# A new order at three seams of an expert layer, and twelve products into a bank that nobody reads

## The chip, the cores and the metric

The kernel runs on one core of a Trainium2 chip. The metric is the device time of one execution in microseconds. Engines are named as in the profile: PE is TensorE, DVE is VectorE, ACT is ScalarE, POOL is GpSimd, SP issues most of the DMAs; ACT and POOL have queues of their own, and POOL's gathers and scatters go through queue q0, SP's transfers through q1.

## The reference, cut to what matters

Three layers follow each other. Attention gives 2304 rows of 512. A mixture of 8 experts then adds to a row, if its skip score is positive, the output of the one expert with the largest gate value:

```python
do_compute = x @ w_skip > 0
xc = x[do_compute]
logits = xc @ w_gate
e_idx = np.argmax(logits, axis=1)
gate_w = probs[np.arange(len(xc)), e_idx]          # probs: softmax of logits
for e in range(E):                                 # E = 8
    mask = e_idx == e
    h = np.maximum(xc[mask] @ w1[e], 0.0)          # 512 x 1024
    y[mask] = gate_w[mask, None] * (h @ w2[e])     # 1024 x 512
out[do_compute] = xc + y
```

A third layer applies `h = x @ w_in; g = h * sigmoid(1.702 h); g @ w_out` to all rows (512 to 2048 to 512).

## The kernel before, in words

All products are made in float16 from two parts: a matrix is scaled by a power of two, its high part is `wh`, the rest `wl`; a product is high by high, low by high and high by low, added up in float32. The same holds for the rows (`xh`, `xl`) and for the hidden values (`hh`, `hl`).

The work has three stages. The first, to about 161 us, is attention in 16 units with the routing behind it: it writes the rows to a table `xd` (L644), the gate values to the same table (L755), and counts for each token the slot in its expert's list (`slots`, L729 to 731; `sa`, L723). A planner (class `Plan`) sets the order of all engines there, SP's among them, from a table of durations and priorities; loads of expert weights are handed to it as `fill`, each with the transfers that it must follow. `in_order` writes the order down as dependencies.

The second stage, to about 335 us, is the experts. For each expert two gathers bring 128 and 64 rows of its list (`gather`, L1017; row numbers `idt` and `idu`, L766 to 769), TensorE transposes them (`xprep`, L1030 and L1033, into `px`), ACT and DVE make `xh` and `xl`, and four blocks each of `l1` (`ph`, L1063) and `l2a`, `l2b` (`py`, L1086, L1101) follow with `l1h`, `l1l` (`hh`, `hl`) between. Each expert's weights are four loads of 1 MB (`load`, L935, key: expert, layer, half). For each half ACT takes a sum of squares (`bound`, `jk`, L951), TensorE adds it over the partitions (`scale`, `psw`, L62), DVE makes the power of two (`scb`, `w_e` to `w_s`, L75 to 81) and then `hi` (`wh`, ACT L975 or DVE L977) and `lo` (`wl`, L983) follow. `ymx`, `yrow`, `yadd` and `scatter` finish the rows.

The order of the second stage on PE, ACT, DVE and POOL is that of one sorted list: each step of expert e stands at e plus a number from the table `STAGE_B`, with exceptions in `head`, `mine` and `tail`, and extra steps that are appended. SP's order comes from the scheduler. Lines on which the change acts:

```python
head = dict(hi00=-6.0, hi01=-5.99, lo00=-5.98)
sched.append((-1.0, -2, 0, lambda e: passes()))
for _, e, i, fn in sorted(sched, key=lambda z: z[:3]):
    fn(e)
```

`passes` counts how many further passes the lists need: a product over the counts (`pc`, L1147), four operations on DVE (`cnt`, `gt`, `sums`, `tot`, L1148 to 1156); `count` reads the result on the engines (L1160) for a branch behind the experts. `xb0` to `xb4` (L774 to 789) find the one scale of all rows (`sx`). `ex.first` keeps the first `lo` behind the row numbers. `win.load`, `win.high`, `win.join` and `win.square` prepare the third layer's first weights beside the experts (ACT `w`, L252; DVE `w`, L231 to 233; ACT `jw`, L256); `win.wh[0]` is ready since the first stage.

The third stage runs from about 338 us to the end.

## Time and profile before

| what | value |
|---|---|
| three runs | 725.91, 728.62, 729.83 us (median 728.62) |
| profiled execution | 728.87 us, its span 727.2 us |
| mean granted clock of TensorE | 0.960 |
| PE busy | 654.9 us (90%) |
| DVE busy | 494.4 us (68%) |
| ACT busy | 425.6 us (59%) |
| POOL busy | 221.5 us (30%) |
| DMA, mean over the span | 131 GB/s |

The span runs from the first to the last instruction of the profiled execution. The granted clock is a share of TensorE's full speed: 1.00 is 2.4 GHz and 0.50 is 1.2 GHz. The busy shares are means over three stages with different limits, so the stretches around the changed places are shown by themselves further down. A release in brackets ("[5.41 <-PE pc L1147]") is the idle time before an instruction and what ended it; "issue" is a wait that the profile does not explain.

### The profile page before, as it was taken

To read this page: it belongs to the slowest core of one execution; us is meant where nothing else is said; L and a number is where in the kernel's file an instruction comes from. 1 tells how busy PE (TensorE), PEld (TensorE's weight loads), DVE (VectorE), ACT (ScalarE), POOL (GpSimd) and SP (SyncE) were. 2 spreads that over 40 slices of the span, in tenths; PEclk is the share of its full clock that TensorE was granted. 3 is DMA by queue.
4 is the path that set the end of the run, shared out by engine and by line. 5 is a ranking of instruction groups with operands and counts; after the bars stand their busy time and mean duration, and the time that the engine had idled before them with its cause. 6 is when DMAs were issued, how large, how long until landed. Compare 5 with 4: busy or idle time off the path is not lost.

```text
span 727.2 us, 16364 instructions
## 1 busy us (share of the span) xinstructions
PE 654.9 (90%) x6639; PEld 460.9 (63%) x6639; DVE 494.4 (68%) x1027; ACT 425.6 (59%) x891; POOL 221.5 (30%) x216
## 2 busy tenths in 40 slices
PE   4788988773889999975999999999999999999997
PEld 3576878663767777753666665444974795695443
DVE  6589898865669999977898999975544365063000
ACT  4478787783785888683779794242544364163111
POOL 6686754205546787781000002411000000000000
PEclk9899999975999999997999999999999999999999
DMA  8799976853747777644240411000011000100111
GB/s 302 235 300 294 280 207 224 274 168 109 234 171 274 247 284 283 216 157 129 76 145 16 174 59 43 16 30 29 16 26 47 16 2 15 29 2 1 30 30 30
DMA packets 37889, 94.90 MB, mean 131 GB/s; under 512 B 8861, under 2 KB 22817, under 8 KB 31668
## 3 DMA queue, kind: packets, MB, share of 16 engines
q1 hardware_dynamic: 34996, 88.34, 37.0%
q0 software_dynamic: 2816, 5.50, 2.5%
q8 instruction: 53, 0.87, 0.5%
q14 instruction: 24, 0.20, 0.1%
HBM read 81.91 MB, written 12.92 MB: 130 GB/s over the span
## 4 chain that ended last, share of the span: by engine, by line
PE 55%; DVE 18%; issue 11%; ACT 6%; DMA 6%; POOL 4%; SPq 0%; POOLq 0%; ACTq 0%; DVEq 0%
PE po L1534 17%; PE ph L1437 13%; PE px L1474 7%; DVE wl L983 3%; PE py L1474 3%; PE ph L1063 3%; DMA xd<-xn 3%; DVE v L1406 2%; PE po L576 2%; POOL ids L1172 2%; PE pz L1474 2%; PE px L628 1%; POOL g L1139 1%; DVE wh L977 1%; PE px L1355 1%
## 5 line engine op out<-in xcount | busy, mean ns | idle before, releaser
L1534 PEld LDWEIGHTS <-gh 128*128 128x128 f16 x576 | 56.2, 98 | 66.4 <-issue 1.3
L983 DVE SCALAR_TENSOR_TENSOR wl<-raw,w_s,wh 128x2048 f16<-128x2048 f32 x32 | 76.5, 2422 | 7.8 <-ACT wh L975 6.9
L1437 PE MATMUL ph<-xx,wih 128*128 128x384 f16 x384 | 72.6, 326 | 0.8 <-ACT xx L1369 0.8
L1542 ACT ACTIVATE o<-po,os 128x128 f32<-128x128 f32 x72 | 20.6, 369 | 83.3 <-issue 55.4
L1534 PE MATMUL po<-woh,gh 128*128 128x512 f16 x288 | 65.9, 379 | 1.0 <-ACT o L1542 1.0
L1534 PE MATMUL po<-wol,gh 128*128 128x512 f16 x288 | 65.6, 379 | 0.0
L1534 PE MATMUL po<-woh,gl 128*128 128x512 f16 x288 | 65.4, 379 | 0.0
L951 ACT ACTIVATE jk<-raw 128x2048 f16<-128x2048 f32 x32 | 61.1, 1911 | 6.4 <-issue 4.9
L1403 POOL TENSOR_TENSOR v<-wih,wil 128x512 f32<-128x512 f16 x16 | 18.4, 1151 | 141.4 <-ACT gh L1429 108.0
L1437 PEld LDWEIGHTS <-wih 128*128 128x128 f16 x384 | 37.7, 100 | 23.9 <-issue 1.0
L1534 PEld LDWEIGHTS <-gl 128*128 128x128 f16 x288 | 28.2, 98 | 33.5
L1063 PEld LDWEIGHTS <-wh 128*128 128x128 f16 x512 | 44.6, 101 | 6.4 <-issue 5.4
L975 ACT ACTIVATE wh<-raw,w_s 128x2048 f16<-128x2048 f32 x18 | 35.2, 1995 | 20.0 <-DVE w_s L80 17.3
L1485 DVE TENSOR_TENSOR q<-pz,q 128x192 f32<-128x192 f32 x24 | 8.6, 358 | 54.7 <-ACT q L1483 49.1
L1437 PE MATMUL ph<-xx,wil 128*128 128x384 f16 x192 | 39.2, 326 | 0.0
L1139 POOL TENSOR_TENSOR g<-g,yr 128x512 f32<-128x512 f32 (+1 forms) x14 | 30.3, 2162 | 26.8 <-ACT yr L1123 26.6
L1441 ACT ACTIVATE sg<-ph,ih 128x384 f32<-128x384 f32 x48 | 27.7, 577 | 17.0 <-PE ph L1437 16.2
L1063 PE MATMUL ph<-xh,wl 128*128 128x192 f16 x256 | 33.2, 253 | 2.8 <-DVE wl L983 1.8
L1430 DVE SCALAR_TENSOR_TENSOR gl<-sg,gs,gh 128x384 f16<-128x384 f32 x48 | 31.0, 646 | 6.3 <-ACT gh L1429 6.0
L1063 PE MATMUL ph<-xl,wh 128*128 128x192 f16 x256 | 33.5, 254 | 1.9 <-DVE xl L1045 1.1
L1474 PEld LDWEIGHTS <-sh 128*128 128x128 f16 x384 | 34.0, 98 | 1.2 <-issue 0.5
L1063 PE MATMUL ph<-xh,wh 128*128 128x192 f16 x256 | 33.5, 255 | 1.2 <-ACT xh L1039 1.0
(262 smaller groups left out, 1649.3 us busy)
## 6 DMA issues: line engine op xcount, KB each, us to landing
raw<-in_moe_w SPq DMA_DIRECT2D x32, 1024.0 KB
vw<-in_vwin SPq DMA_DIRECT2D x16, 576.0 KB
qk<-in_qk SPq DMA_DIRECT2D x16, 576.0 KB
w<-in_moe_w_in SPq DMA_DIRECT2D x8, 1024.0 KB
w<-in_moe_w_out SPq DMA_DIRECT2D x8, 1024.0 KB
vn<-in_v SPq DMA_DIRECT2D x16, 288.0 KB
xd<-xn SPq DMA_DIRECT2D x16, 288.0 KB
x<-xd SPq DMA_DIRECT2D x18, 256.0 KB
```

What stands on the lines that cost most here:

```text
L951: self.nc.scalar.activation(j, r, AF.Square, accum_out=self.mx[i][:, hf, wi:wi + 1])
L975: self.nc.scalar.activation(t, r, AF.Copy, scale=s)
L983: i = self.nc.vector.scalar_tensor_tensor(t, r, s, self.h[e, wi, hf], op0=ALU.mult, op1=ALU.subtract)
L1063: T.matmul(ph[:, fi, :], wa[:, k_, o:o + P], xa[:, k_, :], start=(n == 0), stop=(n == 3 * NK - 1))
L1139: G.tensor_tensor(g, g, yr[e][:, cols(ti)].rearrange("p (h w) -> p h w", w=DM // 2), ALU.add)
L1403: G.tensor_tensor(v, h, l, ALU.add)
L1430: V.scalar_tensor_tensor(split[2], split[0], split[3], split[1], op0=ALU.mult, op1=ALU.subtract)
L1437: T.matmul(ph, win.chunk(wa, f)[:, k_, :], xx[:, k_, :], start=(n == 0), stop=(n == 3 * NK - 1))
L1441: A.activation(sg, ph, AF.Gelu_apprx_sigmoid, scale=ih[:, f // 4:f // 4 + 1])
L1474: T.matmul(o, w[:, k_], xx[:, at + k_], start=(first and i + k_ == 0), stop=(i + k_ == 3), skip_group_check=not first)
L1534: T.matmul(po, ga[:, f, i * P:(i + 1) * P], wa[:, f, :], start=(n == 0), stop=(n == 3 * (DF // P) - 1))
L1542: A.activation(o[:, sl], po[:, sl], AF.Copy, scale=os_[:, j:j + 1])
```

## The change

The step `scale` of the second expert, with `scb`, leaves the first stage's plan. The load with key (1, 0, 1) must follow the last gate writes. `ex.first` is now the last operation of the row scale (`xmax`), and it holds back the first of `hi` and `lo` on DVE, whichever comes first. `passes` stands at -5.97 instead of -1.0. A new step `keep_on` at -6.1 issues twelve products of 128x512 into a PSUM bank that nobody reads. The eight numbers of `win.high` change.

```diff
--- before
+++ after
@@ -766,7 +766,7 @@
         V.tensor_scalar(z, a[:, :, 1, :], 0.0, float(NT + TB), op0=ALU.is_equal, op1=ALU.mult)
         V.scalar_tensor_tensor(z, a[:, :, 1, :], float(TB), z, op0=ALU.mult, op1=ALU.add)
         V.scalar_tensor_tensor(d, z, -float(TB), a[:, :, 0, :], op0=ALU.add, op1=ALU.add)
-        c["idi"] = V.tensor_scalar(d2, d[:, 1, :], 2.0, c["hf2"], op0=ALU.mult, op1=ALU.add).ins
+        V.tensor_scalar(d2, d[:, 1, :], 2.0, c["hf2"], op0=ALU.mult, op1=ALU.add)
         c["id"] = d[:, 0, :], d2
 
     def xb0(u):
@@ -782,11 +782,11 @@
         V.tensor_reduce(t, hd["ps"][0:1, 0:P], axis=AX.X, op=ALU.max)
 
     def xb3(u):
-        T.matmul(hd["ps"][:, P:P + 1], c["onesf"][0:1, :], hd["x0"], start=True, stop=True)
+        c["last_pe"] = T.matmul(hd["ps"][:, P:P + 1], c["onesf"][0:1, :], hd["x0"], start=True, stop=True).ins
 
     def xb4(u):
         c["sx"], c["ix"] = pow2_scale(nc, cp, hd["ps"][:, P:P + 1], "sx", True, t=XT)
-        V.tensor_scalar(c["xmax"], c["ix"], 2.0 ** XT, None, op0=ALU.mult)
+        c["last"] = V.tensor_scalar(c["xmax"], c["ix"], 2.0 ** XT, None, op0=ALU.mult).ins
 
     plan = Plan()
     E0 = [(0, wi, hf) for wi in range(2) for hf in range(2)]
@@ -897,9 +897,8 @@
 
     for i, z in enumerate(sq):
         add(eb, i, [("fill", loads[z])], [("eb",)])
-    for i, rd in ((-1, (0, 1)), (0, (2, 3, 4, 5))):
-        add(es, i, [("eb", j) for j in rd] + ([("xb4", NU - 1)] if i == 0 else []), [("es", "small", 2)])
-        add(ev, i, ["es"], [("ev",)])
+    add(es, -1, [("eb", 0), ("eb", 1)], [("es", "small", 2)])
+    add(ev, -1, ["es"], [("ev",)])
     u = NU - 1
     add(xb0, u, [("xm", i) for i in range(NU)], [("xb0",)])
     add(xb1, u, ["xb0"], [("xbp", "small", 2)])
@@ -968,24 +967,27 @@
             nc.vector.scalar_tensor_tensor(iv, self.s[i, 0][1], ix, self.s[i, 1][1], op0=ALU.mult, op1=ALU.mult)
             self.iv[i] = iv
 
+    def in_turn(self, i):
+        if self.first is not None:
+            self.tc.add_manual_dep(i.ins, self.first.name,
+                                   mybir.DependencyInfo(mybir.DependencyClass.NoSync, mybir.DependencyReason.DATA),
+                                   reason="row numbers and scale first")
+            self.first = None
+
     def hi(self, e, wi, hf, on_act):
         r, s = self.r[e, wi, hf], self.s[e, wi][0]
         t = self.ring.tile([P, r.shape[1], r.shape[2]], F16, tag="h", name="wh")
         if on_act:
             self.nc.scalar.activation(t, r, AF.Copy, scale=s)
         else:
-            self.nc.vector.tensor_scalar(t, r, s, None, op0=ALU.mult)
+            self.in_turn(self.nc.vector.tensor_scalar(t, r, s, None, op0=ALU.mult))
         self.h[e, wi, hf] = t
 
     def lo(self, e, wi, hf):
         r, s = self.r[e, wi, hf], self.s[e, wi][0]
         t = self.ring.tile([P, r.shape[1], r.shape[2]], F16, tag="l", name="wl")
         i = self.nc.vector.scalar_tensor_tensor(t, r, s, self.h[e, wi, hf], op0=ALU.mult, op1=ALU.subtract)
-        if self.first is not None:
-            self.tc.add_manual_dep(i.ins, self.first.name,
-                                   mybir.DependencyInfo(mybir.DependencyClass.NoSync, mybir.DependencyReason.DATA),
-                                   reason="row numbers first")
-            self.first = None
+        self.in_turn(i)
         self.l[e, wi, hf] = t
 
 
@@ -1005,7 +1007,7 @@
     id0, id1 = c["id"]
     sx, ix = c["sx"], c["ix"]
     xdh = xd.rearrange("n (h w) -> (n h) w", h=2)
-    ex.first = c["idi"]
+    ex.first = c["last"]
     ex.onesf, ex.ps = c["onesf"], lambda: psh.tile([P, 512], F32, tag="psh", name="psw")
 
     xg, xs, hts, gv, phs, pxs, pys, yr = {}, {}, {}, {}, {}, {}, {}, {}
@@ -1155,6 +1157,16 @@
         c["tot"] = tot = sm.tile([P, 1], I32, name="tot", bufs=1)
         V.tensor_copy(tot, sums)
 
+    def keep_on(n):
+
+        o = psh.tile([P, 512], F32, tag="psh", name="on")
+        for i in range(n):
+            m = T.matmul(o, c["ones"], win.wh[0][:, 0, 0:512], start=True, stop=True)
+            if "last_pe" in c:
+                tc.add_manual_dep(m.ins, c.pop("last_pe").name,
+                                  mybir.DependencyInfo(mybir.DependencyClass.NoSync, mybir.DependencyReason.DATA),
+                                  reason="order")
+
     def count():
 
         c["passes"] = nc.values_load(c["tot"][0:1, 0:1], min_val=0, max_val=E * c["thr"].shape[1])
@@ -1201,7 +1213,6 @@
     sched = [(max(-9.0, e + STAGE_B[nm]), e, i, nm) for e in range(E) for i, nm in enumerate(fns)]
     head = dict(hi00=-6.0, hi01=-5.99, lo00=-5.98)
     done = [(e, f"{nm}{wi}{hf}") for e, wi in ((0, 0), (0, 1), (1, 0)) for hf in range(2) for nm in ("bound",)]
-    done += [(0, "scale"), (0, "scb")]
     tail = dict(l2b0=-1.23735, l2b1=-1.23734, giv=-1.64, yadd0=-1.22, scatter0=-1.21, ymx=-0.59)
     mine = {**{(0, nm): t for nm, t in head.items()}, (1, "xprep"): -2.3, (1, "xh"): -2.25,
             **{(E - 1, nm): E - 1 + t for nm, t in tail.items()}}
@@ -1212,15 +1223,16 @@
 
     for j, t in zip(range(WA // 2, DF // P // 2), (3.42, 3.43, 4.36, 4.37)):
         word(t, win.load, j, ex.raw1 if j < WA // 2 + 2 else ex.raw)
-    for i, t in zip(range(WA, DF // P), (4.5, 4.51, 4.52, 4.53, 5.1, 5.11, 5.12, 5.13)):
+    for i, t in zip(range(WA, DF // P), (4.891, 4.892, 5.272, 5.273, 5.274, 5.275, 5.39, 5.41)):
         word(t, win.high, i)
     for i, t in zip(range(WA, DF // P), (5.38, 5.4, 5.8, 6.45, 6.46)):
         word(t, win.join, i)
         word(t + 0.05, win.square, i)
     for m in range(2):
         word(5.42 + 0.01 * m, wout.load, 0, m)
-    sched.append((-1.0, -2, 0, lambda e: passes()))
+    sched.append((-5.97, -2, 0, lambda e: passes()))
     sched.append((E - 1 - 0.9, -2, 0, lambda e: count()))
+    sched.append((-6.1, -2, 0, lambda e: keep_on(12)))
     for _, e, i, fn in sorted(sched, key=lambda z: z[:3]):
         fn(e)
     in_order(tc, nb0)
@@ -1689,7 +1701,7 @@
         with ea as s:
             fill = [(6.4, init, "SP", 0.45, 0.1, (), 0), (-7.6, init1, "SP", 1.3, 0.4, [("xd", 0)], 1)]
             fill += [(5.5 + 4 * e + 2 * wi + hf, lambda e=e, wi=wi, hf=hf: [ex.load(e, wi, hf)], "SP", 0.4, 2.75,
-                      [("xd", LOADS_A["e"][4 * e + 2 * wi + hf])] + [("wd", j) for j in range(WA // 2) if e == 0], (e, wi, hf))
+                      [("xd", LOADS_A["e"][4 * e + 2 * wi + hf])] + [("wd", j) for j in range(WA // 2) if e == 0] + [("gs", B - 1)] * (hf == e == 1), (e, wi, hf))
                      for e in range(2) for wi in range(2 - e) for hf in range(2)]
             phase_a(s, tc, c, qk, v, vwin, ex, win, fill, tidy)
         wsm2 = ctx.enter_context(tc.tile_pool(name="wsm2", bufs=1, side="right"))
```

How this stands on the engines: first DVE between the first stage and the first expert. `xb` is the largest value of the rows, `sa`, `idz`, `idt` and `idu` are the row numbers, `wh` and `wl` belong to the first expert's weights. Before:

```order
L774 TENSOR_REDUCE xb<-xm 128x1
L977 TENSOR_SCALAR wh<-raw,w_s 128x2048
L723 TENSOR_TENSOR sa<-sa,sel 128x32
L766 TENSOR_SCALAR idz<-sa 128x16
L767 SCALAR_TENSOR_TENSOR idz<-sa,idz 128x16
L768 SCALAR_TENSOR_TENSOR idt<-idz,sa 128x16
L769 TENSOR_SCALAR idu<-idt,hf_102 128x8
```

And after, in the same place and behind the row scale:

```order
L774 TENSOR_REDUCE xb<-xm 128x1
L723 TENSOR_TENSOR sa<-sa,sel 128x32
L766 TENSOR_SCALAR idz<-sa 128x16
L767 SCALAR_TENSOR_TENSOR idz<-sa,idz 128x16
L768 SCALAR_TENSOR_TENSOR idt<-idz,sa 128x16
L769 TENSOR_SCALAR idu<-idt,hf_102 128x8
...
L789 TENSOR_SCALAR xmax<-sx_i 128x1
L729 SCALAR_TENSOR_TENSOR t_2947<-mn,r_2877 96x6
L983 TENSOR_SCALAR wh<-raw,w_s 128x2048
L730 TENSOR_TENSOR t_2947<-t_2947,cf 96x6
L989 SCALAR_TENSOR_TENSOR wl<-raw,w_s,wh 128x2048
```

`wh` has moved behind the row numbers and behind the row scale; `wl`, which stood two places behind `idu`, follows it.

DVE at the second seam, where the weights of the third expert are split; `giv` is a product of gate value and scales, `cnt` to `tot` are the count of further passes. Before:

```order
L1110 TENSOR_TENSOR giv<-g_3004,iv 128x1
L1110 TENSOR_TENSOR giv<-g_3005,iv 128x1
L1148 COPY cnt<-pc 128x8
L1151 TENSOR_TENSOR gt<-cnt,thr 128x136
L1154 TENSOR_REDUCE sums<-gt 128x1
L1156 CAST tot<-sums 128x1
L1045 SCALAR_TENSOR_TENSOR xl<-px,sx_s,xh 128x768
L983 SCALAR_TENSOR_TENSOR wl<-raw,w_s,wh 128x2048 x2
```

After:

```order
L1112 TENSOR_TENSOR giv<-g_3012,iv 128x1
L1112 TENSOR_TENSOR giv<-g_3013,iv 128x1
L1047 SCALAR_TENSOR_TENSOR xl<-px,sx_s,xh 128x768
L989 SCALAR_TENSOR_TENSOR wl<-raw,w_s,wh 128x2048 x2
```

The four operations have gone to the handover, between the slots and the first `xl`; on PE `pc` went with them, and stands behind the twelve products and ahead of the first transposes.

ACT in the last expert, where `w` are passes over the third layer's weights. Before:

```order
L252 ACTIVATE w_4629<-w_4629 128x512 x2
L252 ACTIVATE w_4631<-w_4631 128x512 x2
L975 ACTIVATE wh<-raw,w_s 128x2048
L1123 ACTIVATE yr<-py,giv 128x512
L1123 ACTIVATE yr<-py,giv 128x256
L1069 ACTIVATE hh<-ph 128x384
L252 ACTIVATE w_4878<-w_4878 128x512 x2
L252 ACTIVATE w_4880<-w_4880 128x512
L1069 ACTIVATE hh<-ph 128x384
L252 ACTIVATE w_4880<-w_4880 128x512
L975 ACTIVATE wh<-raw,w_s 128x2048
```

After:

```order
L981 ACTIVATE wh<-raw,w_s 128x2048
L252 ACTIVATE w_4642<-w_4642 128x512 x2
L1125 ACTIVATE yr<-py,giv 128x512
L1125 ACTIVATE yr<-py,giv 128x256
L1071 ACTIVATE hh<-ph 128x384 x2
L981 ACTIVATE wh<-raw,w_s 128x2048
L252 ACTIVATE w_4644<-w_4644 128x512 x2
L252 ACTIVATE w_4891<-w_4891 128x512 x2
L252 ACTIVATE w_4893<-w_4893 128x512 x2
```

Between the two `wh` stands one pair of `w` passes instead of two; the first `wh` no longer has four ahead of it, and six passes have moved behind the second.

On SP three loads of expert weights have moved from behind the `w_in` load of the first stage to behind the last gate writes, and the read of `tot` (L1160) from behind six loads to behind three.

## Rows read from the trace of the kernel before

**Rows 1.** Table by stretches: window, us, busy (instructions) by engine, clock, DMA share, GB/s

```profile
160.50:176.00 15.50, 3.56 (x29) 3.08 (x29) 8.65 (x30) 8.29 (x11) 5.54 (x4) 0.50 0.28 74
177.50:180.90 3.40, 3.08 (x19) 2.65 (x19) 3.35 (x3) 0.02 (x1) 2.97 (x2) 0.50 0.76 245
187.10:191.10 4.00, 1.99 (x15) 0.92 (x13) 3.13 (x3) 3.05 (x2) 3.39 (x3) 1.00 0.35 72
191.20:194.50 3.30, 3.30 (x21) 2.75 (x21) 2.17 (x2) 2.56 (x4) 2.69 (x3) 0.50 0.69 261
215.00:218.40 3.40, 3.40 (x25) 3.23 (x23) 3.40 (x3) 3.21 (x5) 2.82 (x3) 0.50 0.81 231
232.80:250.20 17.40, 17.40 (x184) 13.60 (x180) 16.55 (x22) 14.65 (x17) 13.79 (x8) 1.00 0.80 255
```

**Rows 2.** Chain of waits, 119 to 146 us: start, length, what

```profile
121.93 12.41 DMA xd<-xn
...
134.40 6.21 DMA xd<-xn
```

**Rows 3.** Waits of ACT, 119 to 146 us: total, times, longest

```profile
ACT xn L638 <- DMA xd<-xn: 1.1, 1, 1.1
```

**Rows 4.** Timeline of SP: start, length, instruction [idle before <-releaser]

```profile
118.93 2.38 SPq L935 DMA_DIRECT2D raw<-in_moe_w  x3
...
176.08 38.75 SPq L935 DMA_DIRECT2D raw<-in_moe_w  x7
```

**Rows 5.** Chain of waits, 160 to 180 us

```profile
161.26 4.72 DMA xd<-gt
```

**Rows 6.** Timeline of DVE, 161 to 187 us

```profile
163.01 0.17 DVE L774 TENSOR_REDUCE xb<-xm 128x1 f32<-128x16 f32 x1 [0.56 <-ACT xj L610]
166.46 1.29 DVE L977 TENSOR_SCALAR wh<-raw,w_s 128x2048 f16<-128x2048 f32 x1 [3.28 <-DMA xd<-gt]
...
168.51 0.23 DVE L769 TENSOR_SCALAR idu<-idt,hf 128x8 int32<-128x8 int32 x1
...
168.92 2.33 DVE L983 SCALAR_TENSOR_TENSOR wl<-raw,w_s,wh 128x2048 f16<-128x2048 f32 x1
```

**Rows 7.** Timeline of POOL, 163 to 183 us

```profile
169.55 2.75 POOL L1017 DMA_INDIRECT g<-xd,idt  x1 [10.59 <-DVE t L729]
172.60 0.95 POOL L1017 DMA_INDIRECT g<-xd,idu  x1 [0.30 <-DVE sx_i L81]
```

**Rows 8.** Timeline of PE, 160 to 187 us

```profile
174.79 1.09 PE L1030 MATMUL px<-ident,g 128*128 128x128 f32 x4 [4.72 <-issue]
```

**Rows 9.** DMA queues, 187.6 to 192 us: packets, MB, share of 16 engines

```profile
q8 instruction: 1, 0.02, 5.9%
```

**Rows 10.** Waits of SP's queue, 162 to 215 us

```profile
SPq L1160 <- DVE tot L1156: 8.6, 1, 8.6
```

**Rows 11.** Timeline of DVE, 203 to 219 us

```profile
204.63 0.22 DVE L1110 TENSOR_TENSOR giv<-g,iv 128x1 f32<-128x1 f32 x2
210.27 0.17 DVE L1148 COPY cnt<-pc 128x8 f32<-128x8 f32 x1 [5.41 <-PE pc L1147]
...
212.13 5.08 DVE L983 SCALAR_TENSOR_TENSOR wl<-raw,w_s,wh 128x2048 f16<-128x2048 f32 x2
```

**Rows 12.** Timeline of PE, 208 to 219 us

```profile
212.26 0.49 PE L1063 MATMUL ph<-xl,wh 128*128 128x192 f16 x4 [0.86 <-DVE xl L1045]
214.53 0.51 PE L1063 MATMUL ph<-xh,wl 128*128 128x192 f16 x4 [1.77 <-DVE wl L983]
```

**Rows 13.** Timeline of ACT, 313 to 333 us

```profile
319.16 1.80 ACT L252 ACTIVATE w<-w 128x512 f32<-128x512 f32 x3
...
321.78 2.00 ACT L975 ACTIVATE wh<-raw,w_s 128x2048 f16<-128x2048 f32 x1
```

**Rows 14.** Timeline of DVE, 313 to 333 us

```profile
323.82 3.08 DVE L983 SCALAR_TENSOR_TENSOR wl<-raw,w_s,wh 128x2048 f16<-128x2048 f32 x1 [1.68 <-ACT wh L975]
```

**Rows 15.** Timeline of PE, 313 to 333 us

```profile
326.95 0.59 PE L1086 MATMUL py<-wl,hh 128*128 128x512 f16 x2 [2.52 <-DVE wl L983]
```

## The prediction

> **What bounds the kernel now.** I read the table of busy time by stretches first, then the chain of waits, then the engines' own timelines around the places where the diff moves something. The reader is to see three kinds of stretch. In the steady middle of the experts TensorE is the bound: 17.40 us of a 17.40 us stretch are busy, at a granted clock of 1.00, VectorE close behind with 16.55 [rows 1]. At the handover from routing to the first expert TensorE works 3.56 of 15.50 us, at clock 0.50, and it is still at 0.50 in 177.50 to 180.90, when products run without a gap [rows 1]. At two seams between experts the clock falls to 0.50 again behind a gap: 191.20 to 194.50 behind 187.10 to 191.10 (1.99 of 4.00 us busy), and 215.00 to 218.40 [rows 1]. What lies before 119 us and behind 335 us is not touched; a gain in between reaches the end whole, since each later stage waits for the earlier one.
>
> **The change part by part.** All times are those of the profiled execution: 728.87 us, 727.2 of it span and 1.67 around it, 0.25 above the median of the three runs (728.62).
>
> *Three loads leave routing.* SP issues three 1 MB loads at 118.93, ahead of the write `xd<-xn` [rows 4]. On the chain that write takes 12.41 us and the next 6.21 [rows 2], and ACT's copy `xn` waits 1.1 us for the second [rows 3]. Without 3 MB ahead of it the write comes many microseconds earlier and this wait goes; VectorE and TensorE behind it move by the same amount. What is late next is the routing arithmetic itself. I take **1.1 us**. Ends: 0 (another wait takes its place) and 2 (twice the wait, should the load behind it also come earlier).
>
> *The loads arrive at the handover.* They now follow the last gate write. In the old kernel that write is 4.72 us on the chain, from 161.26 to 165.98 [rows 5], VectorE's `wh` stands ahead of the row numbers and starts at 166.46 behind it [rows 6], the row numbers end with `idu` at 168.74, and the first gather, 169.55 and 2.75 us long, ends at 172.30, the second at 173.55 [rows 7]. TensorE's first transposes start at 174.79 [rows 8], 2.49 behind the first gather's end; the second gather's rows are then due at 176.04.
> In the new order the row numbers stand right behind `xb`, which ends at 163.18 [rows 6]. In the old trace from `wh`'s end (167.75) to `idu`'s end (168.74) passed 0.99 us [rows 6], so they are ready near 164.2. The gather still waits for the gate write, so it starts near 166.5, at the time at which `wh` may start too (it reuses a buffer that the write reads). A gather that starts under a VectorE pass of this size is longer: 2.75 instead of the second's 0.95, and it ended 1.05 us behind the end of `wl` (168.92 and 2.33 long, so 171.25) [rows 6, 7]. With `wh` at 166.46 to 167.75 the first gather ends near 168.7; the second then runs into `wl` (about 167.95 to 170.3) and ends near 171.3 where it ended at 173.55. Its rows come 2.3 us earlier: **2.3 us**, if landing still takes 2.49.
> The Trainium skill speaks against the new place of `wh` and `wl`: "SBUF — State Buffer", section "SBUF: two separate sides", says that a VectorE operation with two SBUF inputs, or in a two-port mode, holds the port pair shared with GpSimd for its whole length, and descriptors are not written meanwhile. By that rule the first gather could be kept out until `wl` is over too: ends near 171.3 and 172.3, a gain of 1.2 instead of 2.3. The long gather beside `wl` agrees with it.
> Against the gain stands that DMA was 28% busy in 160.50 to 176.00 [rows 1], while 3 MB now go at the same time. The nearest row is `xd<-xn` behind those loads: issued about when the chain enters it at 121.93 it ends at 134.34, so 15.4 us from the loads' issue [rows 2, 4]. Were the gathers held like that, 15.4 us from 161.9 is 177.3, and with 2.49 for their own landing 179.8: 3.8 us later than 176.04. That write lies in the same queue as the loads, the gathers lie in another, so I stay at 2.3; ends -3.8 and +4 (rows written before, landing at once).
> The Trainium skill, "DMA: Bandwidth & Descriptors", section "Queues, rings and completion order", says that an engine takes turns between queues packet by packet. By that the gathers are slowed but do not stand behind 3 MB; no run here shows it for this place.
>
> *Twelve products and one more (`pc`)* stand between `xb`'s small products and the transposes. Two 128x512 products take 0.59 us at full clock [rows 15], so at most 0.30 each, 0.59 at clock 0.50: twelve take up to 7.1 us. They may start when the first scale operation has read the small sum, near 165.3 (one 0.2 us reduction and two small steps behind 164.2), and end by 172.4; the spacing of two in a row, 0.43 us, makes it half that for each and 170.5 in all. The transposes are due at 171 to 173.7. What they could bring is the clock: 3.40 us of products at 0.50 [rows 1] would take 1.7 us at 1.00, and some more of the transposes. What they could cost is 1.3 us if the last of them comes at 172.4 instead of 171.1. They end before the rows land and ACT and VectorE still have to split these, so a gap of a microsecond or more is left. I take **0**, ends -1.3 and +2.1.
> The Trainium skill, "TensorE: Matmul & The Clock Gate", section "HAM oscillation — how this bites in real kernels", tells that a TensorE that waits for data between short pieces of work falls back to the low clock. By that the twelve bring nothing unless the rows follow at once. The clock of 0.50 behind the gap at 187 to 191 agrees [rows 1].
>
> *The total of the rows* moves from the second seam to the handover, and SP's read of it ahead of a load. In the old kernel SP waited 8.6 us for it [rows 10]. It will be ready near 172, and what stands behind it on SP waits for the gathered rows anyway: at 176.08 in the old kernel [rows 4]. **0**; if it were late by 1 us, loads have that much slack.
>
> *The scale of the second expert* moves behind the first `hl` operations: nothing but later weights wait for it, and TensorE has products in hand there. **0**, ends -0.3 and 0.
>
> *The second seam.* VectorE is free at 204.85 and then stands 5.41 us before `cnt`, which waits for `pc` on TensorE; behind it are `xl` and two `wl` (5.08 us from 212.13) [rows 11]. TensorE waits for these, 0.86 and 1.77 us [rows 12], and the clock is 0.50 for 3.40 us afterwards, 1.70 of work at full clock [rows 1]. Without `cnt` in front VectorE starts `xl` at about 204.9 and has both `wl` done by 211.1, before TensorE asks at 212 to 214. 0.86 + 1.77 + 1.70 = **4.3 us**. What is late next is TensorE itself. Ends 2.6 (the clock falls all the same) and 5.
>
> *The last expert.* ACT's second `wh` stands behind three plus one `w` passes: it starts at 321.78 [rows 13]. Between the two `wh` the new order has one pair of passes (1.2 us, by 1.80 for three) in place of four (1.80 and about 0.6). Of the 1.2 us less I take 0.9, since the two `hh` behind the pair wait for products that TensorE ends at its own pace. VectorE's `wl` at 323.82 waits for it 1.68 us [rows 14], and TensorE waits 2.52 us for `wl` [rows 15]. All three move by **0.9 us**, ends 0 (the `hh` hold it) and 1.6 (the wait of VectorE, and no more). The passes that move behind it are done by 326.6, before VectorE needs them.
>
> Sum: 1.1 + 2.3 + 0 + 0 + 0 + 4.3 + 0.9 = 8.6 us. 728.87 - 8.6 = 720.3, and 0.25 less against the median: **720.0 us**. The likeliest case's own range, from half the handover and the tail to a clock that stays up there, is 717 to 723.
>
> **The rivals.**
> - *The slow fetch goes too.* In 187.6 to 192 the queue that brings instructions took 5.9% of 16 engines' 4.4 us, 4.2 us, for one packet [rows 9], just while TensorE has its gaps without a releaser; and the clock fell behind them [rows 1]. If that fetch meets less traffic after the shift, 2.01 of gap, up to 1.65 of clock and a little more go: 4.5 us more, **715.5**. For it: it is the only fetch in a stretch of full DMA. Against: the same loads and gathers of the next experts are shifted with it.
> - *The gathers are held by the loads.* 2.3 turns into -3.8 to 0: 722.3 to 726.1, I take **724**. For it the 12.41 us [rows 2]; against it the other queue.
> - *The second seam is not given back*, because VectorE waits for ACT's `wh` or TensorE for a load: **724.3**. Against it: ACT stands ready by then, as TensorE's waits name VectorE alone [rows 12].
> - *Slower.* The code of TensorE is 24 rows longer ahead of the experts, so its fetches fall at other moments, at 17 us periods in which DMA is 80% busy [rows 1]. One that lands like that at 187 costs some 4.5 us. Two more than now and the gain is gone; three more give **733**. The place is the experts' stage, and three slow fetches there in the new trace decide for it.
> - *The twelve do not lift the clock* is in the forecast; that they do would give 718.
>
> **How the numbers follow.** Forecast 0.48 (with the clock case), slow fetch gone 0.25, gathers held 0.15, seam not given back 0.06, slower or no gain through fetches 0.06. About 0.5% or 3.6 us is what a measurement can tell here: faster is below 725.0. Faster: 0.48 + 0.25 + two thirds of 0.15 + half of 0.06 + 0.01 = 0.87; I lower it to 0.83, since the sum adds five estimates. Same 0.11, slower 0.06. The range must hold the first two and most of the third: 713.5 to 725.5.
>
> **What would show it.** Right: no `xd<-xn` of 12 us and no wait of `xn`; the row numbers near 164 and gathers at 166.5, transposes near 171 to 172; `xl` of the third expert near 201.5 (204.9 less 3.4), with no VectorE wait for `pc`, and clock 1.00 over that seam; `wl` of the last expert 0.9 us earlier against its neighbours. Wrong: gathers' rows landing later than 176, products of the first expert later than before, the second seam's clock at 0.50 still, or TensorE gaps without a releaser at other seams.

## The result, and the profile after

The changed kernel takes 720.55 us (median of 14 runs, 717.16 to 725.88), the kernel before in the same comparison 727.77 us (14 runs, 724.22 to 730.92). The ratio is 0.9904, 95% interval 0.9877 to 0.9930: 7.0 us less, 720.0 was forecast. Ratios leave out runs more than 1.5% above their kernel's fastest, which tells most in e4, where one run of 707.26 us leaves four of ten and not the profiled one. The head of the page:

```profile
span 719.0 us, 16394 instructions
```

The span has shrunk by 8.2 us against the one of before. The table by stretches, with the columns of [rows 1]; the first two are the twelve products and the gap behind them, then the first expert's products, the gap behind the second expert's transposes, and the old place of the second seam:

```profile
163.90:168.30 4.40, 4.32 (x13) 1.58 (x13) 4.11 (x10) 2.02 (x3) 3.28 (x2) 0.64 0.98 391
168.30:173.00 4.70, 0.00 (x0) 0.00 (x0) 1.57 (x9) 1.88 (x1) 3.79 (x4) 0.73 0.83 313
175.60:180.70 5.10, 4.83 (x30) 4.38 (x30) 3.27 (x2) 0.49 (x1) 4.18 (x4) 0.50 1.05 271
186.50:189.60 3.10, 1.43 (x14) 0.85 (x13) 2.28 (x2) 3.01 (x3) 2.79 (x2) 1.00 0.48 25
206.90:224.30 17.40, 17.40 (x184) 13.65 (x182) 16.76 (x22) 14.65 (x18) 14.45 (x9) 1.00 0.87 261
```

The second seam is gone: 206.90 to 224.30 is a whole expert, 17.40 of 17.40 us busy at clock 1.00, where the old kernel had its gap and 3.40 us at 0.50. The handover shows the opposite. While the twelve run the clock rises (mean 0.64), in the gap behind them it falls again (0.73), and the first expert's products stand at 0.50 for 5.1 us, where they stood there for 3.40 us before. The gap with no releaser behind the second expert's transposes (1.99 of 4.00 us busy before) is still there, 1.43 of 3.10, but the clock behind it is 1.00.

The timelines at the handover, first DVE, then POOL, then PE; they answer to [rows 6 to 8]:

```profile
161.68 0.17 DVE L774 TENSOR_REDUCE xb<-xm 128x1 f32<-128x16 f32 x1 [0.73 <-ACT xj L610]
...
162.61 0.23 DVE L769 TENSOR_SCALAR idu<-idt,hf 128x8 int32<-128x8 int32 x1
...
165.07 1.29 DVE L983 TENSOR_SCALAR wh<-raw,w_s 128x2048 f16<-128x2048 f32 x1 [0.15 <-issue]
...
166.40 2.35 DVE L989 SCALAR_TENSOR_TENSOR wl<-raw,w_s,wh 128x2048 f16<-128x2048 f32 x1
```

```profile
164.72 1.77 POOL L1019 DMA_INDIRECT g<-xd,idt  x1 [7.87 <-DVE sx_i L81]
166.79 2.78 POOL L1019 DMA_INDIRECT g<-xd,idu  x1 [0.30 <-DVE t L730]
```

```profile
163.91 4.32 PE L1164 MATMUL on<-wih,ones 128*128 128x512 f16 x12 [0.26 <-DVE sx_e L75]
...
173.08 1.09 PE L1032 MATMUL px<-ident,g 128*128 128x128 f32 x4 [4.84 <-issue]
174.09 0.47 PE L1035 MATMUL px<-ident,g 64*128 64x64 f32 x4
```

The row numbers end at 162.84, 0.99 us behind `xb`'s end, as worked out. Both gathers are done at 166.49 and 169.57, where they ended at 172.30 and 173.55: 5.8 and 4.0 us earlier. But the transposes start at 173.08 and 174.09, only 1.7 and 2.0 us earlier. They stand 6.6 and 4.5 us behind their gather's end in place of 2.49 (the second follow the first without a pause, so their rows may have been there a little sooner). The queues show where the time goes. In 166.5 to 169.7 us, behind the first gather's end, q0, which carries the gathers, has no packet, and q1 with the loads fills the DMA engines; q0's first packets come in 169.7 to 170.7 (packets, MB, share of 16 engines):

```profile
q1 hardware_dynamic: 179, 1.34, 99.7%
```

```profile
q0 software_dynamic: 59, 0.23, 58.2%
```

The second seam on DVE, which answers to [rows 11]: `xl` follows `giv` at once, and both `wl` are done at 208.36, before TensorE asks for them.

```profile
201.91 0.22 DVE L1112 TENSOR_TENSOR giv<-g,iv 128x1 f32<-128x1 f32 x2
202.05 1.01 DVE L1047 SCALAR_TENSOR_TENSOR xl<-px,sx_s,xh 128x768 f16<-128x768 f32 x1
203.74 4.62 DVE L989 SCALAR_TENSOR_TENSOR wl<-raw,w_s,wh 128x2048 f16<-128x2048 f32 x2 [0.68 <-ACT wh L981]
```

The read of `tot` on SP still waits, 7.1 us in place of 8.6, and no wait of TensorE up to the last expert names a load.

The last expert, ACT, DVE and PE ([rows 13 to 15]). One pair of passes stands between the two `wh`. DVE waits 0.45 us for it where it waited 1.68, TensorE 1.79 where it waited 2.52 and 0.95 more. The last row of PE is the third stage's start: 8.12 us of gap where there were 6.41, and its first products stand at clock 0.50, where the old kernel's stood at 1.00 (rows under e2).

```profile
309.29 1.23 ACT L252 ACTIVATE w<-w 128x512 f32<-128x512 f32 x2
...
312.17 1.99 ACT L981 ACTIVATE wh<-raw,w_s 128x2048 f16<-128x2048 f32 x1
```

```profile
314.19 2.35 DVE L989 SCALAR_TENSOR_TENSOR wl<-raw,w_s,wh 128x2048 f16<-128x2048 f32 x1 [0.45 <-ACT wh L981]
```

```profile
316.60 0.59 PE L1088 MATMUL py<-wl,hh 128*128 128x512 f16 x2 [1.79 <-DVE wl L989]
...
329.77 0.37 PE L67 MATMUL psm<-ident,x2m 128*1 128x128 f32 x1 [8.12 <-DVE x2m L1332]
```

### The profile page after: what moved, and what is told of

It is laid out like the page before. It is cut to its first block, busy times and chain, and to the rows that moved or that the text cites. A ratio compares the mean times of both kernels' runs of the same rounds, so it can differ in the third digit from the quotient of the medians.

```text
span 719.0 us, 16394 instructions
## 1 busy us (share of the span) xinstructions
PE 654.4 (91%) x6651; PEld 458.2 (64%) x6651; DVE 493.2 (69%) x1027; ACT 424.9 (59%) x891; POOL 222.4 (31%) x216
## 4 chain that ended last, share of the span: by engine, by line
PE 44%; DVE 6%; issue 2%; ACT 1%; DVEq 0%; ACTq 0%
PE po L1546 17%; PE ph L1449 13%; PE px L1486 7%; PE py L1486 3%; DVE v L1418 2%; PE pz L1486 2%; PE px L1367 1%; DVE sl L1425 1%; DVE v L1419 1%; DVE v L1420 1%; ACT xx L1401 1%; DVE v L1417 0%; ACT o L1554 0%; PE psw L62 0%; DVE xx L1402 0%
## 5 line engine op out<-in xcount | busy, mean ns | idle before, releaser
L1449 PE MATMUL ph<-xx,wih 128*128 128x384 f16 x384 | 74.2, 331 | 0.8 <-ACT xx L1381 0.8
L1546 PEld LDWEIGHTS <-gl 128*128 128x128 f16 x288 | 28.1, 98 | 33.6
L1442 DVE SCALAR_TENSOR_TENSOR gl<-sg,gs,gh 128x384 f16<-128x384 f32 x48 | 29.4, 614 | 11.4 <-ACT gh L1441 11.3
L1184 POOL DMA_INDIRECT ids<-tok,slt x24 | 32.7, 1362 | 7.3 <-issue 6.7
```

Of the source, the lines that this page charges most:

```text
L1184: d = G.indirect_dma_start(c["ids"], IOA(ap=c["slt"][:TB, j:j + 1], axis=0), c["tok"][:TB, j:j + 1], None, bounds_check=RMAX - 1, oob_is_e ...
L1442: V.scalar_tensor_tensor(split[2], split[0], split[3], split[1], op0=ALU.mult, op1=ALU.subtract)
L1449: T.matmul(ph, win.chunk(wa, f)[:, k_, :], xx[:, k_, :], start=(n == 0), stop=(n == 3 * NK - 1))
L1546: T.matmul(po, ga[:, f, i * P:(i + 1) * P], wa[:, f, :], start=(n == 0), stop=(n == 3 * (DF // P) - 1))
```

## The experiments

Each ran beside the kernel before; ratios are to that, with 95% intervals. e1 to e4 ran on one chip, e5 to e12 on another (kernel before: 723.58 us on the first, 726.05 and 726.91 on the second). Since the parts lie in different stretches, their rows tell more than the totals. This table is worked out from the starts of TensorE's products in each profiled execution: the end of routing (its last `sel`), and from there the time to the second expert's transposes, from these to the third expert's, from these to the fifth's, and from the last expert's to the third stage's first product.

| kernel | routing ends | to 2nd expert | 2nd to 3rd | 3rd to 5th | last to third stage |
|---|---|---|---|---|---|
| before | 162.17 | 21.16 | 7.84 | 40.90 | 60.84 |
| e1, count of passes alone | 162.30 | 22.82 | 4.77 | 34.69 | 59.48 |
| e2, tail alone | 158.88 | 22.90 | 4.78 | 39.06 | 58.93 |
| e3, loads alone | 159.77 | 23.42 | 4.78 | 39.10 | 59.98 |
| changed | 160.66 | 21.59 | 7.40 | 34.69 | 59.00 |
| e11, changed again | 158.26 | 21.26 | 7.14 | 34.69 | 58.59 |
| e4, without the twelve | 160.51 | 20.88 | 5.23 | 35.11 | 58.89 |
| e12, the same again | 158.90 | 21.26 | 8.84 | 36.27 | 58.45 |
| e9, twelve of 8 columns | 161.37 | 19.93 | 6.65 | 34.69 | 58.91 |
| e5, 32 products | 159.43 | 18.72 | 12.76 | 35.72 | 58.58 |
| e6, loads behind the rows | 160.20 | 19.82 | 8.59 | 36.24 | 58.40 |
| e10, the same, no products | 162.06 | 21.34 | 10.41 | 35.62 | 58.33 |
| e7, 34 before stage three | 161.40 | 21.70 | 7.08 | 34.69 | 61.69 |
| e8, e6 with 20 and 34 | 156.60 | 18.84 | 10.36 | 37.22 | 61.49 |

**e1: the count of passes alone.**

```diff
-    sched.append((-1.0, -2, 0, lambda e: passes()))
+    sched.append((-5.97, -2, 0, lambda e: passes()))
```

> The kernel before with one edit: the count of further passes (pc on TensorE, cnt to tot on VectorE) stands at the handover. Theory: the second seam alone is worth 4.3 to 4.7 us, so about 723.5 against 728, no wait of VectorE for pc, no wait of TensorE for xl and wl of the third expert, clock 1.00 over that seam. Rival: VectorE or TensorE waits there for something else (ACT's wh, a load) or the clock falls all the same: 1 to 2.6 us, 726 to 727.

0.9946 (0.9909 to 0.9982): 3.9 us, between 1.3 and 6.6. DVE at the seam:

```profile
203.37 0.23 DVE L1110 TENSOR_TENSOR giv<-g,iv 128x1 f32<-128x1 f32 x2
203.51 1.01 DVE L1045 SCALAR_TENSOR_TENSOR xl<-px,sx_s,xh 128x768 f16<-128x768 f32 x1
205.20 2.35 DVE L983 SCALAR_TENSOR_TENSOR wl<-raw,w_s,wh 128x2048 f16<-128x2048 f32 x1 [0.68 <-ACT wh L975]
```

`xl` follows `giv`, and the 5.41 us of [rows 11] are gone. Third to fifth expert takes 34.69 us, all of them busy and at clock 1.00, against 39.06 and 39.10 in e2 and e3, which have the old seam: **4.4 us**. In the old kernel's own profile it is 6.2, since there the clock was still at 0.50 behind the earlier gap. The theory holds.

**e2: the tail alone.** The eight numbers of `win.high`, as in the diff above.

> The kernel before with one edit: the eight numbers of win.high. Theory (prediction): TensorE's wait of 2.52 us for the last expert's wl shrinks by 0.9 us and the end moves by as much. Rival, from the two traces side by side: the tail is worth 1.8 us up to the start of the third stage, since the clock does not fall behind the shorter wait, but the gap in front of the third stage's first small product grows, the clock is at 0.50 for its first products and some 2 us are given back: no change in the end.

0.9983 (0.9943 to 1.0023), not told apart from no change. By the rows there is a gain. PE in e2, then in e1 with the old tail:

```profile
318.37 0.59 PE L1086 MATMUL py<-wl,hh 128*128 128x512 f16 x2 [1.79 <-DVE wl L983]
```

```profile
316.73 0.59 PE L1086 MATMUL py<-wh,hh 128*128 128x512 f16 x2 [0.95 <-ACT wh L975]
319.23 0.59 PE L1086 MATMUL py<-wl,hh 128*128 128x512 f16 x2 [1.91 <-DVE wl L983]
```

1.79 us of waits against 0.95 + 1.91 = 2.86. From the last expert to the third stage, the three kernels of the table with the old tail (before, e1, e3) take 60.1 us in the mean and six with the new one (changed, e2, e4, e9, e11, e12) 58.8: **1.3 us**. The longer gap that the rival foresaw is inside that sum and does not eat it up. What it foresaw of the third stage's first products is a different matter: from there to the end of the span it is 380.8 to 383.7 us in these nine, and the clock at the start tells which. The first 5.80 us of that stage in the kernel before, in the changed kernel, and in the changed kernel again (e11):

```profile
345.58:351.38 5.80, 5.80 (x37) 3.61 (x37) 3.58 (x6) 2.17 (x3) 0.00 (x0) 1.00 0.30 88
```

```profile
335.40:341.20 5.80, 5.80 (x19) 2.76 (x19) 3.47 (x6) 1.25 (x1) 0.00 (x0) 0.50 0.28 80
```

```profile
331.98:337.78 5.80, 5.80 (x37) 3.61 (x37) 3.86 (x7) 2.17 (x3) 0.00 (x0) 1.00 0.28 85
```

At 1.00 from the first product the stage takes 380.8 to 381.6 us (before, e3, e11); where the mean over these 5.80 us is 0.65 or 0.66, 382.7 to 382.8 (e1, e2, e12); at 0.50 to 0.54, 383.4 to 383.7 (changed, e4, e9). The mean is 381.7 for the old tail and 382.9 for the new, but either tail appears both at 1.00 and at 0.65, and two executions of one kernel differ by 2.8 us. So the 1.3 us are shown up to the third stage; that they reach the end is not shown, and the rival stands for that part. e2 still has the old second seam, with this row:

```profile
208.43 0.82 PE L1063 MATMUL ph<-xh,wl 128*128 128x192 f16 x4 [1.80 <-DVE wl L983]
```

**e3: the loads alone.**

```diff
-                      [("xd", LOADS_A["e"][4 * e + 2 * wi + hf])] + [("wd", j) for j in range(WA // 2) if e == 0], (e, wi, hf))
+                      [("xd", LOADS_A["e"][4 * e + 2 * wi + hf])] + [("wd", j) for j in range(WA // 2) if e == 0] + [("gs", B - 1)] * (hf == e == 1), (e, wi, hf))
```

> The kernel before with one edit: the load with key (1, 0, 1), and with it the two behind it, follow the last gate writes. Theory: routing ends 1.1 to 1.5 us earlier, but the first gathers' rows land 4 to 7 us behind their issue in place of 2.5, since 3 MB go beside them; together within 1 us of before. Rival: gathers take turns with the loads, rows land 2.5 to 3 us behind their issue and the gain of routing reaches the end: 1.5 us faster.

0.9979 (0.9943 to 1.0014). The first gather and the first transposes:

```profile
167.78 2.75 POOL L1017 DMA_INDIRECT g<-xd,idt  x1 [11.23 <-DMA raw<-in_moe_w]
```

```profile
172.89 1.12 PE L1030 MATMUL px<-ident,g 128*128 128x128 f32 x4 [3.03 <-DMA g<-xd,idt]
```

The gathers end at 170.53 and 171.78, the transposes start 2.4 and 3.0 us later. Of the landing the theory (4 to 7 us) was wrong and the rival right: in the old order of DVE the gather comes 8 us behind the loads, when these are nearly through. So the loads alone do not delay the rows; the loads and an earlier gather together do.

Routing ends at 159.77; but with the old order it ended at 162.17, 162.30 and 158.88 in three profiled executions, and with the new one in eight (e3, changed, e4, e5, e7, e9, e11, e12) at 158.26 to 161.40, and in e6, e8 and e10, whose loads come later still, at 160.20, 156.60 and 162.06. One order spreads over 3.4 us and more, so a gain of 1.1 can't be read from one profile; the means (161.1 against 160.0) agree with it and do not show it. The wait itself is gone: ACT's `xn` waited 1.1, 1.1 and 0.3 us for the write in the three kernels with the loads there, and not at all in the eleven without.

The three single edits multiply to 0.9946 x 0.9983 x 0.9979 = 0.9908, the whole change is 0.9904: nothing is seen to be left for the handover's order and the twelve, but the intervals would hide some 4 us. DVE's new order with the loads left in routing was not run.

**e4 and e12: without the twelve.**

```diff
-    sched.append((-6.1, -2, 0, lambda e: keep_on(12)))
```

> The changed kernel without the twelve products. Theory: they bring nothing, for TensorE is idle behind them until the rows land and its clock is 0.50 again: the first expert's products run at 0.50 for 3.4 to 5.1 us with and without them, same time within 1 us. Rival 1: without them the clock rises later and the kernel is 1 to 2 us slower. Rival 2: they delay the rise of the clock (5.1 us from the first product of the expert, against 3.4 in the kernel before), and without them it is 0.9 us faster.

> The changed kernel without the twelve, a second time and beside the changed kernel. Theory: 1 to 3 us faster than the changed kernel, under 1 us lost between the second and the third expert's transposes. Rival: the two kernels are the same within 1 us, and the small loss of the first look was chance.

0.9866 (0.9807 to 0.9924; by the medians of all runs 0.9938) and 0.9874 (0.9822 to 0.9925), against 0.9890 (0.9830 to 0.9950) for the changed kernel beside e12, and 0.9904 in the first comparison: the twelve bring nothing that can be measured. Between the second and third expert e4 takes 5.23 us, against 4.77 in e1 to e3, where nothing is lost; the 0.46 between them are the products of the second expert's scale (`psw`), which stand there in the new order, so e4 loses nothing either. That did not come back in e12 (8.84): what I had read from e4 about the twelve's list was chance, and e12's rival, the same kernel within 1 us, comes nearest.

**e5: 32 products.** `keep_on(32)` for `keep_on(12)`.

> The changed kernel with 32 in place of twelve products at the handover, so that TensorE works until about 172.5 us, just ahead of the first transposes at 173.1. Theory: what undid the twelve is the gap of 4.8 us behind them; with 32 the clock is 1.00 when the rows land and the first expert's products run at 1.00 from their start: 2.5 us less up to the second expert's transposes. Rival: the waits of 1 us between transposes and products are enough for the clock to fall: no change. Cost if the rows land earlier: up to 1 us.

0.9915 (0.9865 to 0.9966). PE at the handover, and the table by stretches from 167 us on:

```profile
163.22 8.39 PE L1164 MATMUL on<-wih,ones 128*128 128x512 f16 x32 [0.25 <-DVE sx_e L75]
...
173.46 0.49 PE L1065 MATMUL ph<-xh,wh 128*128 128x192 f16 x4 [1.04 <-ACT xh L1041]
```

```profile
167.00:171.50 4.50, 4.50 (x23) 1.98 (x22) 1.53 (x5) 2.05 (x3) 3.77 (x3) 1.00 0.84 314
171.50:175.00 3.50, 1.89 (x20) 1.53 (x19) 2.47 (x6) 0.90 (x1) 2.71 (x3) 1.00 0.79 205
175.00:178.00 3.00, 3.00 (x40) 3.00 (x38) 1.72 (x1) 0.00 (x0) 2.39 (x3) 1.00 0.93 343
```

The clock is 1.00 from 167 to 178 us, also through the 1.04 us that TensorE waits for `xh`, and the first expert's products take 4.69 us to the second's transposes at 178.15, where they took 6.64. So the gap behind the twelve undid them, as the theory says. But 2nd to 3rd expert takes 12.76 us: 8 us lost, part of them because the clock is at 0.50 again from 186.4 us, with such rows on PE:

```profile
187.77 0.32 PE L1065 MATMUL ph<-xh,wl 128*128 128x192 f16 x1 [0.62 <-issue]
188.47 0.32 PE L1065 MATMUL ph<-xh,wh 128*128 128x192 f16 x1 [0.38 <-issue]
```

One or a few products every 0.7 us, inside one accumulation, with no releaser. The gain is more than given back there.

**e6: the loads behind the first rows.** The three loads wait for the first expert's gathers, and the sum of squares of one moves on ACT behind `xh`. The part of the edit that holds the loads back:

```diff
-                ex.last.setdefault((1, 1, 0), []).append(d)
+                for z in ((1, 1, 0), (1, 0, 1), (2, 0, 0), (2, 0, 1)):
+                    ex.last.setdefault(z, []).append(d)
```

> The changed kernel, but the three loads wait for the first expert's rows, as the load with key (1, 1, 0) does; the sum of squares of the load (1, 0, 1) moves behind xh on ACT. Theory: the rows land 2.5 us behind the gathers' end again (first transposes near 169 to 171 in place of 173.1), 2 to 4 us of the handover come back; if the second expert's weights then come late, part of it is lost at its first products. Rival: the landing of 4.5 to 6.6 us is not the loads' doing, and the transposes stay at 172 to 173.

0.9941 (0.9898 to 0.9984). POOL and PE:

```profile
165.66 1.52 POOL L1019 DMA_INDIRECT g<-xd,idt  x1 [8.68 <-issue]
167.48 1.87 POOL L1019 DMA_INDIRECT g<-xd,idu  x1 [0.30 <-issue]
```

```profile
169.84 0.63 PE L1033 MATMUL px<-ident,g 128*128 128x128 f32 x4 [1.27 <-issue]
171.75 0.44 PE L1036 MATMUL px<-ident,g 64*128 64x64 f32 x4 [1.29 <-DMA g<-xd,idu]
```

The gathers end at 167.18 and 169.35, the transposes start 2.66 and 2.40 us later, in place of 6.6 and 4.5. **The late landing is the loads' doing**, shown by taking them away. It repeats: q0's first packet starts 2.3 to 3.3 us behind the first gather's end in the seven executions with the loads under way and DVE's new order (changed, e4, e5, e7, e9, e11, e12), and 0.7 us behind it in the other seven (before, e1 to e3, e6, e8, e10). The second expert's transposes come 1.8 us sooner behind routing (19.82 against 21.59), and the stretch behind them takes that back: 8.59 against 7.40, and 1.55 us more from the third to the fifth, at low clock in part. In e10, with the same loads, they come no sooner (21.34) than in e4 and e12.

**e9 and e10: what sets the loss behind the second expert's transposes.** e9 cuts the twelve to 8 columns (the edit below), e10 is e6 without the twelve, e11 is the changed kernel again.

```diff
-            m = T.matmul(o, c["ones"], win.wh[0][:, 0, 0:512], start=True, stop=True)
+            m = T.matmul(o[:, 0:8], c["ones"], win.wh[0][:, 0, 0:8], start=True, stop=True)
```

> The changed kernel with the twelve products cut to 8 columns each: as many instructions on TensorE's list, a tenth of the work. Two theories of the place behind the second expert's transposes, where TensorE gets one to three products every 0.71 us with no releaser and the five profiled kernels with such products lost 2.3 to 8 us between the second and the third expert's transposes, that without them 0.5. Theory A (list): the 24 further instructions put that place where their supply is late; this kernel loses 2 us or more there, as the changed kernel does. Theory B (time): the sooner TensorE comes there, the longer it waits; this kernel loses as little as the one without the twelve, under 1 us.

> The changed kernel with the three loads behind the first rows and without the twelve products. Theory A (list): no further instructions, so no loss between the second and the third expert's transposes, and the 2 us of the handover that the late loads bring reach the end: about 3 us under the kernel without the twelve, 714 to 717. Theory B (time): TensorE is 2 us earlier there, waits 2 us or more, and the third expert's transposes stand 26 to 28 us behind the routing's last products as before; end as without the twelve.

> The changed kernel, a second time, to see what of its rows repeats: 0.987 to 0.994 of the kernel before; routing's last products between 158 and 162 us; 2 to 3 us lost between the second and the third expert's transposes by theory A, between 0 and 4 by theory B, as its execution comes there.

0.9851 (0.9767 to 0.9935), 0.9921 (0.9887 to 0.9955) and 0.9890 (0.9830 to 0.9950). Against 4.77 us e9 takes 1.9 us more, e10 5.6, e11 2.4, each with the 0.46 of `psw` in it. e10 comes to 720.7 us and not to 714 to 717. Theory A (list) falls: e10 and e12 have no product more than the old kernel and take 5.6 and 4.1 us more. Theory B (time) fares little better: the three executions that came to the second expert latest (22.82 to 23.42 us behind routing) lost nothing, and ten of the eleven that came sooner (18.72 to 21.70) lost something; but e4 came at 20.88 and lost nothing, e9 at 19.93 and takes 1.9 more, e10 at 21.34 and takes 5.6 more. The packets of the instruction queue q8 do not fit either: in e10 TensorE stands so from 188.2 to 192.8 us and there is none from 178 to 192.8, and e3 has one of 2.4 us at 186.7 and loses nothing. **What holds TensorE there stays open.**

**e7 and e8: products ahead of the third stage.** e7 has 34 more products behind the last expert's, e8 has these, 20 at the handover and e6's loads.

```diff
+    sched.append((99.0, -2, 0, lambda e: keep_on(34)))
```

> The changed kernel with 34 further products that nobody reads behind the last expert's, in TensorE's gap of 8.1 us ahead of the third stage. Theory: the clock is 1.00 when that stage begins; 12 transposes and 24 products of its start, 8 us at 0.50 in the changed kernel, take half of the time where they do not wait for loads: 2 to 3 us less. Rival: the gap of 0.75 us between the two small products, and the waits for rows, let the clock fall again: no change, or slower by what the scheduler's other order in the third stage costs.

> The changed kernel with the loads behind the first rows, 20 products at the handover and 34 ahead of the third stage. Theory: the gains of the three add: 4 to 8 us under the changed kernel, 712 to 716. Rival: the clock falls in each place all the same and the second expert's weights come late: 718 to 722.

0.9981 (0.9942 to 1.0020) and 1.0013 (0.9974 to 1.0052): both worse than the changed kernel. PE in e7:

```profile
331.65 0.27 PE L67 MATMUL psm<-ident,x2m 128*1 128x128 f32 x1 [2.14 <-ACT jw L256]
333.37 1.97 PE L1368 MATMUL px<-ident,x 128*128 128x128 f32 x8 [1.45 <-DMA x<-xd]
335.27 0.58 PE L69 MATMUL psm<-x2m,onesf 1*128 1x1 f32 x2
```

With other instructions ahead the scheduler put eight transposes, which wait 1.45 us for rows, between the two small products that the row scale hangs on: 3.62 us from the first to the second, where it was 1.13. The stage starts 2.8 us later behind the last expert's products. Nor did the clock hold: it was 1.00 when the 34 ended at 329.5, and 0.50 from 331.9 through the first 3.6 us of the stage's products (338.6 to 342.2). So both halves of the rival came true. What a start at 1.00 would be worth is seen by itself in the rows under e2: 2.8 us between two executions of the changed kernel. e8 loses by the same, and 5.6 us between the second and third expert. No version that I ran beats the changed kernel beyond its interval.

## Why the prediction was right, point by point

The time, the range and the sign were right. Of the seven terms of the sum one carries the result, one is right up to the third stage, and the largest of the others is wrong. That 720.55 lies so near to 720.0 is in part luck: the gain was put at 8.6 and is 7.0, the kernel before was 0.85 us faster in this comparison than in the three runs that the forecast starts from, and the changed kernel's own two profiles lie 6.2 us apart (719.0 and 712.8 of span).

- **Second seam, 4.3 us: right**, 4.4 between e1 and its neighbours in the table, by the mechanism named, and 3.9 in e1's whole time.
- **Last expert, 0.9: right in kind**, 1.3 measured. The term took the earlier `wh` alone; TensorE's two waits of 0.95 and 2.52 became one of 1.79, and part of it is given back in a longer gap ahead of the third stage, which the prediction had not priced. Nor need a gain ahead of that stage reach the end whole, as the prediction has it: by the clock at its start the stage takes 380.8 to 383.7 us, and in the profiled pair the changed kernel's takes 2.0 us longer than the old one's.
- **Loads out of routing, 1.1: mechanism shown, size not resolved.** The wait of `xn` for the write is gone in all eleven kernels without the loads, but routing's end spreads by 3.4 us within one order.
- **Handover, 2.3: wrong**, and the step that failed is "if landing still takes 2.49". The gathers ended earlier than worked out; the transposes came at 173.08 and not at 171 to 172. The prediction stayed at 2.3 because the gathers lie in another queue than the loads, and that did not keep them free. Turns between the queues, on which it counted, would have slowed the gathers only; but with the loads under way their first packet started 2.3 to 3.3 us behind the first gather's end (else 0.7), 9.0 to 9.5 us behind the loads' issue, when q1 had 0.1 to 0.2 MB left to move. So the rival of gathers held by the loads had the mechanism right, for nearly all of the 3 MB, and only its price wrong: 15.4 us behind the loads' issue by its row, 9.4 in the changed kernel (160.37 to 169.8), which made the rows 2 to 4 us late. What was left of the gain was taken back one expert later: from routing's end to the third expert's transposes the old order took 27.6 to 29.0 us (before, e1, e2, e3; mean 28.1), the new one with its loads 26.1 to 30.1 (changed, e4, e7, e9, e11, e12; mean 28.2). The term is not told apart from 0, with single executions 4 us apart.
- **Twelve products, 0: right, for the reason given**: the gap behind them undoes the clock (0.64, 0.73, then 0.50), and e5 shows that without the gap it stays at 1.00.
- **The scale of the second expert, 0, ends -0.3 and 0: a little low.** Its `psw` stand between the second and third expert now and take TensorE 0.46 us there (e4). **The total of the rows, 0: right**, no wait of TensorE names what stands behind it.
- **The slow fetch**: forecast to stay, with a chance of 0.25 to go. The gap stayed, the clock behind it did not fall, some 1.6 us less. The cause that I named, one long packet of instructions, is not borne out. One 4.2 us packet filled the gap in [rows 9]; in the changed kernel the packet at the same place is short:

```profile
q8 instruction: 1, 0.02, 4.9%
```

4.9% of 16 engines over 1.4 us is 1.1 us, and TensorE takes 2.6 us longer than in e1 to e3, 0.46 of it for `psw`; in e10 it stands so with no such packet at all.
- **Slower through the stream**: a stall of this kind is real in its place (up to 8 us in e5), but not three times over, and that fetches make it is not shown.

In sum 4.4 + 1.3 and an unresolved 1.1 are 6.8 us, beside 7.0 measured (interval 5.1 to 9.0). Only the 4.4 are tied to a cause up to the end; the rest fits and is not resolved. The forecast's 8.6 had the handover's 2.3 too much and the tail's 0.4 too little.

## What to carry to other kernels

An operation that waits for a late result costs what stands behind it on its engine: moving four tiny ones to where their engine was idle gave most of this change. A gather that is issued earlier is not rows that land earlier; ask what else DMA carries in the same microseconds, and look at the landing, not the issue. Before crediting a gain at one place, add up to the next point where all engines meet, over several executions: here the handover's gain was not to be seen one expert later, and the tail's hung on the clock at which the next stage began.

## What the runs showed that was not expected

- A gather that runs into a large pass of VectorE ends a nearly fixed time behind it. In the changed kernel the second ended 0.82 us behind `wl` (169.57 against 168.75), and it did so in all ten kernels with that order (0.81 to 0.82); in the four with the old order it was 1.04 for the first. `wh` holds the first gather in the same way: 1.4 to 2.0 us long, it ended 0.12 to 0.13 us behind `wh` in the six executions in which it began before `wh` or with it (166.49 against 166.36 in the changed kernel), and 1.03 in the four in which it began 0.5 us or more behind `wh`'s start. The Trainium skill, "SBUF — State Buffer", section "SBUF: two separate sides", which has GpSimd kept out for a whole VectorE operation (one with two SBUF inputs only against a GpSimd operation that reads SBUF, as the gather reads its row numbers), is borne out in kind. The prediction's further step, that the first gather could be kept out until `wl` is over too, did not come.
- With 32 products the clock stayed at 1.00 through later waits of about a microsecond; with twelve and a gap of 4.8 us it did not.
- Between the second and third expert TensorE lost 1.4 to 7.5 us in ten of fourteen executions, getting one to three products every 0.7 us with no releaser, and two executions of one kernel differ by 3.6 us in it. With routing's spread of 3.4 us and the third stage's of 2.8, both within one kernel or one order, that is as large as most edits here.
